# Attention and FFN on one core: score maxima on a finer grid and four units later, weight-conversion words in an idle output bank

## The chip, the cores and the metric

The kernel runs on one core of one Trainium2 chip. The metric is the time of the device for one execution, in microseconds (us). The kernel before was timed three times; the median counts. The profile is one execution, recorded by the hardware profiler.

## The reference

Attention over 4 batches of 8 heads, 768 tokens and 64 dimensions, in which a query sees only the keys of its hash bucket, and then an FFN over the 3072 tokens. Cut to what matters:

```python
q_bits = (einsum('bhsd,dk->bhsk', q, proj) > 0)          # 6 hash bits, k_bits the same
mask   = q_bucket[:, :, :, None] == k_bucket[:, :, None, :]
scores = where(mask, scale * q @ k.T, -1e9)
attn   = exp(scores - max(scores)); attn /= attn.sum() + 1e-9
x = (attn @ v).reshape(3072, 512)
h = x @ w_in                                            # 512 -> 2048
g = where(h >= 1, h, where(h <= -1, 0, (h + 1) ** 2 / 4))
out = g @ w_out                                         # 2048 -> 512
```

## The kernel before, in words

The 32 heads go one after another. A head has 12 units: two halves of 384 queries, each against six tiles of 128 keys. The mask is made part of the product: beside the parts of q and k the operand T2 holds rows for the hash bits and a row for the maximum, so that a score comes out of two matmuls (`s_unit`, L371 and L372) into one of four score tiles `s` in PSUM. Only the second, L372, reads T2. ScalarE takes the exponential twice (ph rounded, L380, and full, L385), and `lo_unit` subtracts them for the low part pl (L39), on VectorE, or on GpSimd (POOL) for units 0, 3, 6 and 9 of a head. Four units later `pv_unit` adds three matmuls with v (L404, L405, L406) into an output bank: bank 0 for the first half of a head (TensorE is at units 4 to 9 of the head), bank 1 for the second (units 10 to 15, the last four of which are units 0 to 3 of the next head). After the last unit of a half ScalarE copies the bank to xs (L412).

**Maxima.** For each head `max_mm` multiplies a tile of 128 rows of T2 with all 768 columns in a pair of matmuls (L310) into the one `smax` tile, which takes two banks of PSUM; VectorE reduces it (L314) to a column of nm. The next pair waits for that. A head has six pairs. In the loop a pair stands at the end of a unit, and its maximum follows the score matmuls of the next unit. From head 4 on there is a pair at the end of each even unit, for the head two ahead; the ends of the early pairs are in a table. When a head's six columns are there, `max_clamp` clamps nm in two steps on GpSimd (L342, L344), `max_tr` transposes it on TensorE into an output bank (L349), and `max_put` copies the result to te on ScalarE (L354) and sends it in two DMAs of SP's queue: into the row of T2 (L356) and to memory (L357). This happens in the head just before the one that reads the row: clamp at its unit 0, transpose at 4, copy and DMA at 5. Head 2 alone does it by halves of the queries (`half_clamp` on VectorE, `half_put`, L333 and L337).

**Hash bits.** For each pair of heads `bits_mm` (L210) makes two times four matmuls, one set in each output bank, ScalarE negates (L216), VectorE compares (L221), GpSimd scales, and at unit 18 of the pair `bits_put` sends four DMAs on SP's queue (L282) into T2.

**Weight conversion.** 24 pieces of the FFN's weights, 128x512 numbers of 64 bits each, are turned into float32 halves, one in each of heads 3 to 26 (`WeightSplit.steps`): a DMA (L62), a square on ScalarE (L69), and integer steps on VectorE, which build a word in the tile `wa` in SBUF: L70 (one input), L74, L78 (wraw and the word), L82 (the square times the word). Then a cast (L87), a subtraction and a DMA (L95). The offsets in `conv` set the unit of each step within the head.

All of it is one order of the program; each engine and SP's queue work through their instructions in that order. `tasks` holds what `at(unit, ...)` put at the end of a unit. Then comes the FFN, which this change does not touch: its weights keep `wa` in SBUF.

Of the kernel before, what the change touches and what calls it, by code (L numbers as in the profile page):

```python
# [41 lines left out]
class WeightSplit:  # L42
# [7 lines left out]
        nc.vector.memset(sc[:, 1:2], 29)  # L50
        self.sc = sc

    def steps(self, src, shape, hi, lo, cp, stage=None, low=None, keep=None):
        nc, n = self.nc, self.n
        st = {}

        def s0():
            st["raw"] = self.pool.tile([P, n, 2], I32, name="wraw")
            dst = st["raw"]
            if len(shape) == 4:  # L60
                dst = dst.rearrange("p (c f) t -> p c f t", c=shape[1])
            nc.sync.dma_start(out=dst, in_=src)  # L62

        def s1():
            raw = st["raw"]
            sq = st["sq"] = self.pool.tile([P, n], F32, name="wsq")
            a = st["a"] = self.pool.tile([P, n], I32, name="wa", bufs=1)
            high = raw[:, :, 1].bitcast(F32)
            nc.scalar.activation(out=sq, in_=high, func=AF.Square)  # L69
            nc.vector.tensor_scalar(out=a, in0=raw[:, :, 1], scalar1=0x07FFFFFF, scalar2=3,  # L70
                                    op0=ALU.bitwise_and, op1=ALU.logical_shift_left)

        def s2():
            nc.vector.scalar_tensor_tensor(out=st["a"], in0=st["raw"][:, :, 1], scalar=self.sc[:, 0:1],  # L74
                                           in1=st["a"], op0=ALU.bitwise_and, op1=ALU.bitwise_or)

        def s3():
            nc.vector.scalar_tensor_tensor(out=st["a"], in0=st["raw"][:, :, 0], scalar=self.sc[:, 1:2],  # L78
                                           in1=st["a"], op0=ALU.logical_shift_right, op1=ALU.bitwise_or)

        def s4():
            nc.vector.scalar_tensor_tensor(out=st["sq"], in0=st["sq"], scalar=WMIN2,  # L82
                                           in1=st["a"].bitcast(F32), op0=ALU.is_ge, op1=ALU.mult)
# [25 lines left out]
POOL_J = (0, 3)  # L109
PV_ORDER = (1, 2, 0, 4, 5, 3)  # L110
NU = 2 * NJ


def attention(ctx, tc, wst, T1, T2, qk, v, pj, cv, x_d, s_d, e_d, tasks, shared):
# [4 lines left out]
    shared["work"], shared["small"] = work, small  # L119
    ps_s = ctx.enter_context(tc.tile_pool(name="ps_s", bufs=4, space=PSUM))  # L120
    ps_o = ctx.enter_context(tc.tile_pool(name="ps_o", bufs=1, space=PSUM))
    ps_m = ctx.enter_context(tc.tile_pool(name="ps_m", bufs=1, space=PSUM))
# [138 lines left out]
                             start=True, stop=True)  # L261

    def row_half(hd, hf, bank=None):
        ps = ps_m.tile([P, 2, 512], F32, name="smax")[:, 0] if bank is None else obank[bank]
# [56 lines left out]
    def half_clamp(hd, hf):  # L321

        nm = nms[hd]
        x = nm[:, hf * HB:(hf + 1) * HB]
        nc.vector.tensor_scalar(out=nmh[:, hf, HB:2 * HB], in0=x, scalar1=CLAMP, scalar2=None, op0=ALU.is_gt)
        nc.vector.tensor_scalar(out=nmh[:, hf, 0:HB], in0=x, scalar1=CLAMP, scalar2=None, op0=ALU.min)

    def half_put(hd, hf, bank):
        pr, h = hd // 2, hd % 2
        if hf == 1:  # L330
            nms.pop(hd)
        ps = obank[bank]
# [4 lines left out]
        nc.sync.dma_start(out=T2[pr % NQK][7:8, 0, h, sl].bitcast(F32), in_=te[0:HB].bitcast(F32))  # L337
        nc.sync.dma_start(out=e_d[hd // H][hd % H:hd % H + 1, sl], in_=te[HB:2 * HB].bitcast(F32))
# [5 lines left out]
        eng.tensor_scalar(out=nm[:, 0:NJ], in0=nm[:, 0:NJ], scalar1=CLAMP, scalar2=None,  # L344
                          op0=ALU.min)

    def max_tr(hd, bank):
        ps = mx[hd] = obank[bank]
        nc.tensor.transpose(out=ps[0:2 * NJ, 0:P], in_=nms.pop(hd), identity=ident)  # L349

    def max_put(hd):
# [40 lines left out]

    xss = {}

    def pv_unit(n):
        hd, hf, jj = n // NU, (n % NU) // NJ, n % NJ
        j = PV_ORDER[jj]
        pr, h = hd // 2, hd % 2
# [3 lines left out]
        wa = va[:, j, h:h + 2, :].rearrange("p g d -> p (g d)")  # L402
        wb = vb[:, j, h:h + 2, :].rearrange("p g d -> p (g d)")
        nc.tensor.matmul(out=o, lhsT=wa, rhs=ph, start=(jj == 0), stop=False)  # L404
        nc.tensor.matmul(out=o, lhsT=wb, rhs=ph, start=False, stop=False)  # L405
        nc.tensor.matmul(out=o, lhsT=wa, rhs=pl, start=False, stop=(jj == NJ - 1))  # L406
        if jj == NJ - 1:
            if hf == 0:
# [121 lines left out]

    for t in (1, 0):
        at(0, first_scale, 1, t, nc.gpsimd)
    at(9, ones_row, 1, nc.vector)
    at(3, row_clamp, 0, NJ // 2, NJ)
    at(4, row_half, 0, 1, 1)
    for n, g in enumerate((1, 4, 5, 6)):
        at(g, quarter, n)
    at(6, lambda: nc.gpsimd.memset(T2[1][0:64, 0].bitcast(F32), 0.0))
    at(7, row_clamp, 1, 0, NJ // 2)
    for n in (0, 1):  # L540
        at(8, move, 1, n)
    at(8, bits_mm, 1, 0, 1)
    at(9, bits_cmp, 1, 0)
    at(9, row_half, 1, 0)
    at(9, row_flags, 0)
    at(10, bits_mm, 1, 1, 0)
# [54 lines left out]

    NG = NH * NU
    red = None
    early = {}
    for hd, gs in ((0, (0, 2)), (1, (4, 5, 6, 8, 11, 12)), (2, (15, 16, 17, 19, 20, 22)),
                   (3, (21, 23, 24, 26, 27, 29)), (4, (30, 31, 33, 34, 35, 37)),
                   (5, (38, 39, 41, 42, 44, 46))):
        early.update({n: (hd, NJ - len(gs) + i) for i, n in enumerate(gs)})
    for g in range(NG + LAG + 1):
        if g < NG:  # L610
            s_unit(g)
        if red is not None:
            max_red(*red)
            red = None
        if 1 <= g <= NG:
            lo_unit(g - 1)
        if g < 4 * NU:
            due = g in early
            hd, i = early.get(g, (0, 0))
        else:  # L620
            hd, i = g // NU + 2, g % NU // 2
            due = hd < NH and g % 2 == 0
        if g >= LAG and g - LAG < NG:
            pv_unit(g - LAG)
        if due:
            max_mm(hd, 2 * i)
            max_mm(hd, 2 * i + 1)
            red = (hd, i)
        for fn, a in tasks.pop(g, ()):
            fn(*a)  # L630
    for g in sorted(tasks):
        for fn, a in tasks[g]:
            fn(*a)
# [465 lines left out]
def lsh_attn_ffn(ctx: ExitStack, tc: tile.TileContext, qk, v, pj, cv, w_in, w_out, out):  # L1099
# [46 lines left out]
    def conv(g, steps, offs):  # L1146
        for fn, n in zip(steps, offs):
            at(g + n, fn)

    def wi_steps(i, cp, stage=None):  # L1150
        return ws.steps(win_v[:, :, i * P:(i + 1) * P, :], (P, NCT, P, 2), wih[i], wil[i], cp, stage, None, wq[i])

    def wo_steps(i, cp, stage=None, low=None):
        return ws.steps(wout_v[i], (P, DM, 2), woh[i], wol[i], cp, stage, low)
# [21 lines left out]
    attn = {}  # L1176
# [107 lines left out]
```

## Time and profile before

| | us |
|---|---|
| three runs | 980.84, 982.14, 981.41 |
| median | 981.41 |
| span of the profiled execution | 980.2 |
| TensorE busy in it | 966.7 |
| VectorE busy | 793.9 |
| ScalarE busy | 679.6 |
| GpSimd busy | 346.3 |

The profiled execution has a span of 980.2 us; its own time is one of the three runs' kind, between 980.84 and 982.14, so that about a microsecond lies around the span. The attention stage lasts to about 463 us, the FFN follows. In the rows PE is TensorE's matmuls, PEld its weight loads, DVE VectorE, ACT ScalarE, POOL GpSimd, SP SyncE. A row of a timeline gives start, duration, engine, line, operation, out<-in, and in brackets the idle time ahead with what ended it. A row of the waits gives who waited for whom, the total in us, how often, and the longest. A row of the groups gives count, busy time and the mean of one in ns.

### The profile page before, as it was taken

To read this page: it belongs to the slowest core of one execution; us is meant where nothing else is said; L and a number is where in the kernel's file an instruction comes from. 1 tells how busy PE (TensorE), PEld (TensorE's weight loads), DVE (VectorE), ACT (ScalarE), POOL (GpSimd) and SP (SyncE) were. 2 spreads that over 40 slices of the span, in tenths; PEclk is the share of its full clock that TensorE was granted. 3 is DMA by queue.
4 is the path that set the end of the run, shared out by engine and by line. 5 is a ranking of instruction groups with operands and counts; after the bars stand their busy time and mean duration, and the time that the engine had idled before them with its cause. 6 is when DMAs were issued, how large, how long until landed. Compare 5 with 4: busy or idle time off the path is not lost.

```text
span 980.2 us, 15590 instructions
## 1 busy us (share of the span) xinstructions
PE 966.7 (99%) x5050; PEld 889.7 (91%) x5050; DVE 793.9 (81%) x1359; ACT 679.6 (69%) x1481; POOL 346.3 (35%) x418
## 2 busy tenths in 40 slices
PE   8999999999999999999999999999999999999998
PEld 7889999999999999999999998888988889988886
DVE  8779999999999999887898887877866777655554
ACT  7878988898899898888655555455564545544444
POOL 8767777778887777666000000000000000000000
PEclk9999999999999999999999999999999999999999
DMA  6674667676666667644395478966458554454431
GB/s 164 178 189 108 165 175 184 192 180 192 168 159 162 177 174 187 161 119 126 126 319 185 129 237 287 314 223 205 116 157 240 149 183 119 143 159 119 117 88 65
DMA packets 95113, 167.56 MB, mean 171 GB/s; under 512 B 13956, under 2 KB 51960, under 8 KB 95032
## 3 DMA queue, kind: packets, MB, share of 16 engines
q1 hardware_dynamic: 94808, 166.56, 59.6%
q8 instruction: 40, 0.66, 0.3%
q14 instruction: 41, 0.34, 0.1%
q10 hardware_dynamic: 224, 0.00, 0.0%
HBM read 106.13 MB, written 33.87 MB: 143 GB/s over the span
## 4 chain that ended last, share of the span: by engine, by line
PE 87%; DVE 5%; ACT 3%; DMA 2%; issue 1%; POOL 1%; SPq 1%; DVEq 0%; ACTq 0%; POOLq 0%
PE y L822 27%; PE h L1054 18%; PE smax L310 7%; PE h L959 7%; PE o L406 5%; PE o L404 5%; PE o L405 5%; PE s L371 5%; PE s L372 5%; DVE nm L314 2%; PE o L210 2%; DVE pl L39 1%; DMA wraw<-in_w_in_dram 1%; ACT ph L380 1%; DMA sm<-sd 0%
## 5 line engine op out<-in xcount | busy, mean ns | idle before, releaser
L380 ACT ACTIVATE ph<-s 128x384 fp32r<-128x384 f32 x380 | 188.3, 496 | 41.1 <-PE s L372 35.1
L314 DVE TENSOR_REDUCE nm<-smax 128x1 f32<-128x768 f32 x189 | 179.0, 947 | 15.2 <-PE smax L310 13.6
L39 POOL TENSOR_TENSOR pl<-pf,ph 128x384 fp32r<-128x384 f32 x128 | 141.9, 1112 | 87.8 <-ACT pf L385 83.1
L787 DVE SCALAR_TENSOR_TENSOR t<-t 128x384 f32<-128x384 f32 x128 | 71.3, 557 | 101.6 <-ACT z L782 101.3
L39 DVE TENSOR_TENSOR pl<-s,ph 128x384 fp32r<-128x384 f32 x256 | 135.8, 544 | 10.8 <-ACT s L385 9.6
L371 PE MATMUL s<-t 128*128 128x384 f32 x384 | 132.2, 344 | 0.0
L404 PE MATMUL o<-ph,va 128*128 128x386 f32 x384 | 130.1, 339 | 1.1 <-DVE neg L221 1.1
L406 PE MATMUL o<-pl,va 128*128 128x386 f32 x384 | 130.1, 339 | 0.4 <-DVE pl L39 0.4
L405 PE MATMUL o<-ph,vb 128*128 128x386 f32 x384 | 130.1, 339 | 0.0
L372 PE MATMUL s<-t 128*128 128x384 f32 x384 | 129.3, 337 | 0.0
L385 ACT ACTIVATE s<-s 128x384 f32<-128x384 f32 x252 | 125.2, 497 | 0.0
L822 PE MATMUL y<-t,ghi 128*128 128x512 f32 x384 | 124.7, 395 | 0.0
L310 PE MATMUL smax<-t 128*128 128x384 f32 x378 | 103.1, 354 | 5.7 <-DVE nm L314 4.4
L781 ACT ACTIVATE t<-h,mh 128x384 f32<-128x384 f32 x56 | 32.6, 581 | 84.0 <-PE h L959 44.3
L310 PEld LDWEIGHTS smax<-t 128*128 128x128 f32 x378 | 64.4, 188 | 23.8 <-DVE nm L314 22.1
L792 ACT CAST ghi<-z 128x384 fp32r<-128x384 f32 x129 | 65.1, 505 | 30.1 <-DVE z L788 26.3
L782 ACT ACTIVATE z<-t,m 128x384 f32<-128x384 f32 x128 | 79.0, 617 | 4.2
L1054 PE MATMUL h<-wbig,t 128*128 128x384 f32 x399 | 81.4, 336 | 0.0
L822 PEld LDWEIGHTS y<-t,ghi 128*128 128x128 f32 x384 | 71.3, 188 | 11.1 <-ACT ghi L792 0.3
L1054 PEld LDWEIGHTS h<-wbig,t 128*128 128x128 f32 x399 | 71.6, 188 | 5.3
L781 ACT ACTIVATE t<-wsq,mh 128x384 f32<-128x384 f32 x48 | 29.6, 617 | 67.0 <-DVE wsq L1067 40.8
L822 PE MATMUL y<-t,glo 128*128 128x512 f32 x192 | 76.0, 396 | 0.0
(189 smaller groups left out, 2134.9 us busy)
## 6 DMA issues: line engine op xcount, KB each, us to landing
t<-wc SPq DMA_DIRECT2D x92, 256.0 KB
t<-t SPq DMA_DIRECT2D x60, 384.0 KB
wraw<-wc SPq DMA_DIRECT2D x76, 256.0 KB
raw<-in_qk_dram SPq DMA_DIRECT2D x14, 768.0 KB
wraw<-in_w_in_dram SPq DMA_DIRECT2D x16, 512.0 KB
wraw<-in_w_out_dram SPq DMA_DIRECT2D x16, 512.0 KB
t<-ed SPq DMA_DIRECT2D x36, 192.0 KB
xd<-xs SPq DMA_DIRECT2D x32, 192.5 KB
```

What stands on the lines that cost most here:

```text
L39: eng.tensor_tensor(out=out, in0=a, in1=b, op=ALU.subtract)
L310: nc.tensor.matmul(out=smax[hd][:, hf, 0:HS], lhsT=t2[:, 0, h, i * P:(i + 1) * P], rhs=t2[:, 1, h, hf * HS:(hf + 1) * HS], start=True, sto ...
L314: nc.vector.tensor_reduce(out=nmp(hd)[:, i:i + 1], in_=smax[hd][:, :, 0:HS], axis=AX.XY, op=ALU.max, negate=True)
L371: nc.tensor.matmul(out=ps[:, 0:HS], lhsT=t1[:, 1, h, ks], rhs=t1[:, 0, h, sl], start=True, stop=False)
L372: nc.tensor.matmul(out=ps[:, 0:HS], lhsT=t2[:, 1, h, ks], rhs=t2[:, 0, h, sl], start=False, stop=True)
L380: nc.scalar.activation(out=ph[:, 0:HS], in_=ps[:, 0:HS], func=AF.Exp, scale=SCALE)
L385: nc.scalar.activation(out=pf, in_=ps[:, 0:HS], func=AF.Exp, scale=SCALE)
L404: nc.tensor.matmul(out=o, lhsT=wa, rhs=ph, start=(jj == 0), stop=False)
L405: nc.tensor.matmul(out=o, lhsT=wb, rhs=ph, start=False, stop=False)
L406: nc.tensor.matmul(out=o, lhsT=wa, rhs=pl, start=False, stop=(jj == NJ - 1))
L822: nc.tensor.matmul(out=ys[c][m], lhsT=g_[:, m * P:(m + 1) * P], rhs=w, start=(first and k == 0), stop=(last and k == 2))
L1054: nc.tensor.matmul(out=ps, lhsT=w[:, cs], rhs=x, start=(n == 0 and s not in (2, 3, 6)), stop=(n == 5), skip_group_check=True)
```

## The change

Five things, in one step:

- The word of the conversions is no longer the tile `wa` in SBUF but output bank 0, read as integers, for the pieces that are converted in the attention stage. The bank is idle from unit 10 to 15 of a head, so the steps move: L70 and L74 to unit 10, L78 to 12, L82 to 14; the later steps one unit earlier.
- The hash products of a pair, from the third pair on, move from units 7 (bank 1) and 11 (bank 0) to units 5 and 7, both in bank 1.
- The pairs of the maxima of heads 1 to 5 are placed by slots, five to a unit (a slot is a score or output matmul), so that a pair may stand in the middle of a unit: heads 2 to 5 every 7.7 slots. From head 6 on they stay at the end of even units, four units later than before.
- Clamp, transpose and copy follow: from head 5 on at units 3, 6 and 7 of the head before; heads 2 to 4 go by halves, clamped on GpSimd. The transposes go into a score tile and no longer into an output bank.
- Two small moves at the start: `ones_row(1)` behind the first hash compare, `row_clamp(1)` one unit later.

The core of the diff:

```diff
-    def steps(self, src, shape, hi, lo, cp, stage=None, low=None, keep=None):
+    def steps(self, src, shape, hi, lo, cp, stage=None, low=None, keep=None, word=None):
...
-            a = st["a"] = self.pool.tile([P, n], I32, name="wa", bufs=1)
+            a = st["a"] = self.pool.tile([P, n], I32, name="wa", bufs=1) if word is None else word()
...
+    shared["work"], shared["small"], shared["word"] = work, small, lambda: obank[0].bitcast(I32)
...
-        nc.vector.tensor_scalar(out=nmh[:, hf, HB:2 * HB], in0=x, scalar1=CLAMP, scalar2=None, op0=ALU.is_gt)
-        nc.vector.tensor_scalar(out=nmh[:, hf, 0:HB], in0=x, scalar1=CLAMP, scalar2=None, op0=ALU.min)
+        nc.gpsimd.tensor_scalar(out=nmh[:, hf, HB:2 * HB], in0=x, scalar1=CLAMP, scalar2=None, op0=ALU.is_gt)
+        nc.gpsimd.tensor_scalar(out=nmh[:, hf, 0:HB], in0=x, scalar1=CLAMP, scalar2=None, op0=ALU.min)
...
-    def max_tr(hd, bank):
-        ps = mx[hd] = obank[bank]
+    def max_tr(hd, bank=None):
+        ps = mx[hd] = ps_s.tile([P, 512], F32, name="s") if bank is None else obank[bank]
...
+        between(3)
         nc.tensor.matmul(out=o, lhsT=wb, rhs=ph, start=False, stop=False)
+        between(4)
...
-    at(9, ones_row, 1, nc.vector)
...
+    at(9, ones_row, 1, nc.vector)
...
-    at(18, half_clamp, 2, 0)
-    at(19, half_put, 2, 0, 1)
-    at(23, half_clamp, 2, 1)
-    at(25, half_put, 2, 1, 0)
+    for hd, gs in ((2, (19, 21, 24, 26)), (3, (29, 31, 34, 36)), (4, (38, 40, 43, 45))):
+        for n, g in enumerate(gs):
+            at(g, half_put if n % 2 else half_clamp, hd, n // 2)
...
-        if 0 < hd < NH - 2:
-            gc, gt = ((g + NU + 6, g + NU + 7) if hd == 1 else (g + NU + 2, g + NU + 4) if hd == 2
-                      else (g + NU, g + NU + 4))
-            at(gc, max_clamp, hd + 2, nc.gpsimd if hd > 2 else nc.vector)
-            at(gt, max_tr, hd + 2, 1)
-            at(gt + (hd > 1), max_put, hd + 2)
+        if 2 < hd < NH - 2:
+            at(g + NU + SHIFT - 1, max_clamp, hd + 2, nc.gpsimd)
+            at(g + NU + SHIFT + 2, max_tr, hd + 2)
+            at(g + NU + SHIFT + 3, max_put, hd + 2)
...
-            bits_at = ((20, 1), (23, 0)) if pr == 0 else ((8 if pr == 1 else 7, 1), (11, 0))
+            bits_at = (((20, 1), (23, 0)), ((8, 1), (11, 0)))[pr] if pr < 2 else ((5, 1), (7, 1))
...
+    places = [5, 15] + [25, 33, 40, 48, 55, 62] + [80 + 77 * n // 10 for n in range(4 * NJ)]
...
+        early.update({5 * ((hd - 2) * NU + SHIFT + 2 * i + 1): (hd, i) for i in range(NJ)})
...
+        def between(k):
+            if 5 * g + k in early:
+                hd, i = early.pop(5 * g + k)
+                max_mm(hd, 2 * i)
+                max_mm(hd, 2 * i + 1)
+                if k == 5:
+                    return hd, i
+                max_red(hd, i)
...
-        conv((2 * i + 3) * NU, wi_steps(i, nc.scalar), (0, 7, 9, 13, 15, 17, 19, 21))
+        conv((2 * i + 3) * NU, wi_steps(i, nc.scalar), (0, 10, 10, 12, 14, 16, 18, 20))
...
-        conv((4 + 2 * n) * NU, first, (0, 7, 9, 13, 15, 16))
+        conv((4 + 2 * n) * NU, first, (0, 10, 10, 12, 14, 15))
```

`SHIFT` is 4. The order shows what this does to two engines. First VectorE in head 11, before: L314 is a maximum, pl the low parts, wa the word of the conversion.

```order
L70 TENSOR_SCALAR wa_2485<-wraw_2381 128x512
L39 TENSOR_TENSOR pl_6_168<-s_2474,ph_6_161 128x384
L314 TENSOR_REDUCE nm_2394<-smax_2497 128x1
L39 TENSOR_TENSOR pl_0_162<-s_2488,ph_0_155 128x384
L74 SCALAR_TENSOR_TENSOR wa_2485<-wraw_2381,wsc_108,wa_2485 128x512
L314 TENSOR_REDUCE nm_2394<-smax_2523 128x1
L39 TENSOR_TENSOR pl_2_164<-s_2514,ph_2_157 128x384
L39 TENSOR_TENSOR pl_3_165<-s_2526,ph_3_158 128x384
L314 TENSOR_REDUCE nm_2560<-smax_2546 128x1
L78 SCALAR_TENSOR_TENSOR wa_2485<-wraw_2381,wsc_108,wa_2485 128x512
```

The same place after (all lines in the changed file are up to six higher: L315 is the maximum, L70 to L82 are the same; o0 is output bank 0):

```order
L315 TENSOR_REDUCE nm_2457<-smax_2505 128x1
L39 TENSOR_TENSOR pl_0_162<-s_2496,ph_0_155 128x384
L70 TENSOR_SCALAR o0_137<-wraw_2395 128x512
L74 SCALAR_TENSOR_TENSOR o0_137<-wraw_2395,wsc_108,o0_137 128x512
L315 TENSOR_REDUCE nm_2457<-smax_2530 128x1
L39 TENSOR_TENSOR pl_2_164<-s_2521,ph_2_157 128x384
L39 TENSOR_TENSOR pl_3_165<-s_2537,ph_3_158 128x384
L78 SCALAR_TENSOR_TENSOR o0_137<-wraw_2395,wsc_108,o0_137 128x512
L315 TENSOR_REDUCE nm_2457<-smax_2557 128x1
L39 TENSOR_TENSOR pl_5_167<-s_2565,ph_5_160 128x384
L82 SCALAR_TENSOR_TENSOR wsq_2533<-wsq_2533,o0_137 128x512
L315 TENSOR_REDUCE nm_2457<-smax_2586 128x1
```

L70 and L74 now stand side by side ahead of one maximum, and L78 and L82 stand ahead of the next two.

Second SP's queue at the end of head 10 and in head 11, before: xd and sd take the finished output of a head, te is the row of the maxima, bits the hash bits.

```order
L416 DMA xd1_60<-xs_2336 64x770
L417 DMA sd1_64<-xs_2336 1x768
L95 DMA wq15_96<-wsq_2298 128x512
L356 DMA t2_0_77<-te_2453 1x6x128
L357 DMA ed1_68<-te_2453 6x128
L282 DMA t2_1_78<-bits_2308 8x768 x4
L62 DMA wraw_2549<-in_w_out_dram 128x1024
```

After (L419 is L416, L357 is L356, L283 is L282):

```order
L419 DMA xd1_60<-xs_2352 64x770
L420 DMA sd1_64<-xs_2352 1x768
L95 DMA wq15_96<-wsq_2368 128x512
L283 DMA t2_1_78<-bits_2282 8x768 x4
L357 DMA t2_0_77<-te_2492 1x6x128
L358 DMA ed1_68<-te_2492 6x128
L62 DMA wraw_2561<-in_w_out_dram 128x1024
```

The row of the maxima has moved from ahead of the four transfers of the hash bits to behind them.

More of the change, by code (lines that the diff above doesn't have):

```diff
@@ L111 @@
 NU = 2 * NJ
+SHIFT = 4
 def attention(ctx, tc, wst, T1, T2, qk, v, pj, cv, x_d, s_d, e_d, tasks, shared):
@@ L118, in attention @@
     small = ctx.enter_context(tc.tile_pool(name="asmall", bufs=2))
-    shared["work"], shared["small"] = work, small
+    shared["work"], shared["small"], shared["word"] = work, small, lambda: obank[0].bitcast(I32)
     ps_s = ctx.enter_context(tc.tile_pool(name="ps_s", bufs=4, space=PSUM))
@@ L263, in row_half @@
     def row_half(hd, hf, bank=None):
-        ps = ps_m.tile([P, 2, 512], F32, name="smax")[:, 0] if bank is None else obank[bank]
+        ps = ps_s.tile([P, 512], F32, name="s") if bank is None else obank[bank]
         row_mm(hd, hf, ps)
@@ L324, in half_clamp, with half_put @@
         x = nm[:, hf * HB:(hf + 1) * HB]
-        nc.vector.tensor_scalar(out=nmh[:, hf, HB:2 * HB], in0=x, scalar1=CLAMP, scalar2=None, op0=ALU.is_gt)
-        nc.vector.tensor_scalar(out=nmh[:, hf, 0:HB], in0=x, scalar1=CLAMP, scalar2=None, op0=ALU.min)
-    def half_put(hd, hf, bank):
+        nc.gpsimd.tensor_scalar(out=nmh[:, hf, HB:2 * HB], in0=x, scalar1=CLAMP, scalar2=None, op0=ALU.is_gt)
+        nc.gpsimd.tensor_scalar(out=nmh[:, hf, 0:HB], in0=x, scalar1=CLAMP, scalar2=None, op0=ALU.min)
+    def half_put(hd, hf):
         pr, h = hd // 2, hd % 2
@@ L331, in half_put @@
             nms.pop(hd)
-        ps = obank[bank]
+        ps = ps_s.tile([P, 512], F32, name="s")
         nc.tensor.transpose(out=ps[0:2 * HB, 0:P], in_=nmh[:, hf], identity=ident)
@@ L393, in attention, with pv_unit @@
     xss = {}
-    def pv_unit(n):
+    def pv_unit(n, between):
         hd, hf, jj = n // NU, (n % NU) // NJ, n % NJ
@@ L538, in attention @@
     at(6, lambda: nc.gpsimd.memset(T2[1][0:64, 0].bitcast(F32), 0.0))
-    at(7, row_clamp, 1, 0, NJ // 2)
+    at(8, row_clamp, 1, 0, NJ // 2)
     for n in (0, 1):
@@ L603, in attention @@
     red = None
[L604 to L608, printed above, removed]
-    for g in range(NG + LAG + 1):
+    order = [(0, 4), (0, 5)] + [(hd, i) for hd in range(1, 6) for i in range(NJ)]
+    places = [5, 15] + [25, 33, 40, 48, 55, 62] + [80 + 77 * n // 10 for n in range(4 * NJ)]
+    early = {n + (n % 5 == 1): hi for n, hi in zip(places, order)}
+    for hd in range(6, NH):
+        early.update({5 * ((hd - 2) * NU + SHIFT + 2 * i + 1): (hd, i) for i in range(NJ)})
+    for g in range(NG + LAG + 1):
+        def between(k):
[6 more added lines that the diff above has]
+                max_red(hd, i)
         if g < NG:
@@ L613, in attention @@
             max_red(*red)
-            red = None
         if 1 <= g <= NG:
             lo_unit(g - 1)
[L617 to L622, printed above, removed]
-        if g >= LAG and g - LAG < NG:
[L624 to L628, printed above, removed]
+        between(2)
+        if g >= LAG and g - LAG < NG:
+            pv_unit(g - LAG, between)
+        red = between(5)
         for fn, a in tasks.pop(g, ()):
             fn(*a)
+    assert not early
     for g in sorted(tasks):
@@ L1148, in conv, with word @@
             at(g + n, fn)
+    attn = {}
+    def word():
+        return attn["word"]()
     def wi_steps(i, cp, stage=None):
-        return ws.steps(win_v[:, :, i * P:(i + 1) * P, :], (P, NCT, P, 2), wih[i], wil[i], cp, stage, None, wq[i])
+        return ws.steps(win_v[:, :, i * P:(i + 1) * P, :], (P, NCT, P, 2), wih[i], wil[i], cp, stage, None, wq[i], word)
     def wo_steps(i, cp, stage=None, low=None):
-        return ws.steps(wout_v[i], (P, DM, 2), woh[i], wol[i], cp, stage, low)
+        return ws.steps(wout_v[i], (P, DM, 2), woh[i], wol[i], cp, stage, low, None, None if stage is None else word)
     woh = [hi for hi, lo in wo]
@@ L1175, in lsh_attn_ffn @@
     actx = ExitStack()
-    attn = {}
     for b in range(B - 1):
```

## The prediction

> **What bounds the kernel now.** I read the page first (busy time and the chain that ended last), then the waits of TensorE's weight loads in three stretches of the attention stage, then the timelines of one head. The page, busy time of each engine and the chain's share by engine:
>
> ```profile
> PE 966.7 (99%) x5050; PEld 889.7 (91%) x5050; DVE 793.9 (81%) x1359; ACT 679.6 (69%) x1481; POOL 346.3 (35%) x418
> ```
>
> ```profile
> PE 87%; DVE 5%; ACT 3%; DMA 2%; issue 1%; POOL 1%; SPq 1%; DVEq 0%; ACTq 0%; POOLq 0%
> ```
>
> TensorE is the bound; the change adds no matmul and removes none. It can only win back, or add, time in which TensorE waits. The waits of its weight loads, by line and releaser (total, times, longest), first from 14 to 79.6 us, then to 399.6, then to 463:
>
> ```profile
> PEld smax L310 <- DVE nm L314: 9.4, 17, 1.4
> PEld o L404 <- DVE neg L221: 1.4, 1, 1.4
> PEld smax L310 <- POOL t L247: 0.8, 1, 0.8
> ```
>
> ```profile
> PEld smax L310 <- DVE nm L314: 11.6, 39, 0.4
> PEld smax L310 <- DVE sm L666: 0.5, 1, 0.5
> ```
>
> ```profile
> PEld o L349 <- issue: 0.4, 1, 0.4
> ```
>
> Nearly all is one wait: a pair of score matmuls (L310) needs the only smax tile, which VectorE's maximum (L314) must have read. One head in detail, head 5 around its unit 10. VectorE, start and duration, whole stretch:
>
> ```profile
> 104.96 0.96 DVE L314 TENSOR_REDUCE nm<-smax 128x1 f32<-128x768 f32 x1
> 105.83 0.55 DVE L39 TENSOR_TENSOR pl<-s,ph 128x384 fp32r<-128x384 f32 x1
> 106.30 1.58 DVE L74 SCALAR_TENSOR_TENSOR wa<-wraw,wsc,wa 128x512 int32<-128x512 int32 x1
> 107.80 0.94 DVE L314 TENSOR_REDUCE nm<-smax 128x1 f32<-128x768 f32 x1
> 108.67 1.00 DVE L39 TENSOR_TENSOR pl<-s,ph 128x384 fp32r<-128x384 f32 x2
> 109.60 0.94 DVE L314 TENSOR_REDUCE nm<-smax 128x1 f32<-128x768 f32 x1
> 110.47 1.01 DVE L78 SCALAR_TENSOR_TENSOR wa<-wraw,wsc,wa 128x512 int32<-128x512 int32 x1
> ```
>
> The two pairs on TensorE in the same stretch, and the weight load of the second:
>
> ```profile
> 106.51 0.51 PE L310 MATMUL smax<-t 128*128 128x384 f32 x2
> ...
> 108.80 0.62 PE L310 MATMUL smax<-t 128*128 128x384 f32 x2
> ```
>
> ```profile
> 108.80 0.30 PEld L310 LDWEIGHTS smax<-t 128*128 128x128 f32 x2 [0.35 <-DVE nm L314]
> ```
>
> A pair can issue 0.06 after the maximum ends (108.74, 108.80). Unhindered, twelve matmuls stand from one pair to the next, 2.11 us, so the second was due at 108.62: it came 0.18 late and ran 0.11 longer. The word step L74 (1.58 here) sat ahead of the maximum. The wait listed at 0.35 cost TensorE 0.29, so I take 0.8 of the 12.1 us in the middle stretch, 9.7 us, as what its 23 conversion heads lose now, 0.42 each; and 0.9 of the early 11.6, 10.4 us.
>
> **The change part by part.** *Words in the output bank.* The four word steps now write PSUM (L82 reads it), and the first two stand together ahead of the maximum of unit 10. Their rows now (steady heads, then the later stage where GpSimd is idle; count, total, mean ns):
>
> ```profile
> L39 DVE TENSOR_TENSOR pl<-s,ph 128x384 fp32r<-128x384 f32 x184 | 96.9, 542 | 4.2 <-ACT s L385 4.2
> L78 DVE SCALAR_TENSOR_TENSOR wa<-wraw,wsc,wa 128x512 int32<-128x512 int32 x23 | 25.7, 1116 | 0.0
> L74 DVE SCALAR_TENSOR_TENSOR wa<-wraw,wsc,wa 128x512 int32<-128x512 int32 x24 | 25.2, 1050 | 0.0
> L82 DVE SCALAR_TENSOR_TENSOR wsq<-wsq,wa 128x512 f32<-128x512 f32 x23 | 24.8, 1080 | 0.0
> ```
>
> ```profile
> L221 DVE TENSOR_TENSOR neg<-o,neg 32x384 f32<-32x384 f32 x23 | 12.4, 541 | 5.7 <-ACT neg L216 5.7
> ```
>
> ```profile
> L74 DVE SCALAR_TENSOR_TENSOR wa<-wraw,wsc,wa 128x512 int32<-128x512 int32 x8 | 6.0, 752 | 0.3
> ```
>
> Beside a busy GpSimd L74, with two inputs in SBUF, takes 1050; alone it takes 752. The subtraction pl, with one input in PSUM, takes 542 beside the same GpSimd. So I expect 0.75 for each of L74, L78 and L82, three times 0.33 off VectorE per head. The Trainium skill's page "SBUF — State Buffer" (section "Who interferes with whom") says just this: two SBUF inputs contend with a GpSimd read, at most one does not; the rows above agree.
>
> How fast one follows another, from the later stage:
>
> ```profile
> 504.54 0.68 DVE L39 TENSOR_TENSOR wol<-wsq,woh 128x512 fp32r<-128x512 f32 x1
> 505.14 0.42 DVE L70 TENSOR_SCALAR wa<-wraw 128x512 int32<-128x512 int32 x1
> 505.60 0.75 DVE L74 SCALAR_TENSOR_TENSOR wa<-wraw,wsc,wa 128x512 int32<-128x512 int32 x1
> 506.27 0.62 DVE L846 SCALAR_TENSOR_TENSOR pcs<-tmp,xsvb,pcs 128x384 f32<-128x384 f32 x1
> ```
>
> From L70 to L74 0.46 us, from L74 to the next 0.67. L70 into PSUM is nowhere in the trace. Its ends: 0.46, if it stays as fast; 0.72, if it takes the 0.68 of L39 on as many elements and its 0.04 to the dependent step. I take 0.60, between them. The Trainium skill's page "VectorE: DVE Perf Modes" (section "Why PSUM operands drop a tier") says that a PSUM operand holds fp32 work to the plain rate; by it L70 would be at the 0.72 end and the sum 2.8 us higher. No run here shows it yet.
>
> L70 also gets a wait: the bank is free only when ScalarE has copied out the finished half of the head. That copy:
>
> ```profile
> 106.13 0.48 ACT L412 COPY xs<-o 128x384 f32<-128x384 f32 x1
> ```
>
> ends at 106.61, while VectorE is through with pl at 106.30. Behind the waiting L70 stand L74 and the maximum, and behind that TensorE's next pair. The walk, with the rows' times: L70 at 106.65, L74 at 107.25, maximum 107.91 to 108.87, pair at 108.93 where 108.62 was due: 0.31 late, and 0.1 for its longer run. Then VectorE is free at 108.78 (the next step starts 0.87 after a maximum's start), two pl take 0.93, L78 0.66, maximum 110.37 to 111.33, pair at 111.39 where 111.14 was due: 0.25 and 0.1. Then one pl, L82 and a maximum to 113.4, ahead of 113.6: no wait. That is 0.76 per head. In the heads that start a pair of heads, the second hash compare (L221, 0.54) now stands ahead of the maximum of unit 8, so that VectorE is later at L70; between 0 and 0.3 more, I take 0.14. Twelve odd heads at 0.76 and eleven even ones at 0.90 make 19.0 us against 9.7: **+9.3**. With L70 at its ends the odd heads pay 0.62 or 0.88: the total moves by -3.2 or +2.8.
>
> *The rows of the maxima.* From head 5 on, clamp, transpose and copy come later; for the transpose it is two units, 2.1 us. What follows it is ScalarE's copy te and two small transfers on SP's queue, and in odd heads the hash bits' four transfers now stand ahead of these. ScalarE, SP and TensorE in head 7:
>
> ```profile
> 129.77 0.25 ACT L354 CAST te<-o 12x128 fp32r<-12x128 f32 x1
> ```
>
> ```profile
> 130.05 0.77 SPq L356 DMA_DIRECT2D t<-te  x1
> ...
> 131.42 3.60 SPq L282 DMA_DIRECT2D t<-bits  x4
> ```
>
> ```profile
> 135.81 0.34 PE L372 MATMUL s<-t 128*128 128x384 f32 x1
> ```
>
> The row is issued 5.8 us ahead of the matmul that reads it. Two units later it would be 3.7 ahead; behind the bits' 3.6 us, if those start at 129.4, where SP is free, it is issued at 133.0, 2.8 ahead. The least that the trace shows to be in time:
>
> ```profile
> 396.34 1.54 SPq L356 DMA_DIRECT2D t<-te  x1
> ```
>
> ```profile
> 400.07 0.34 PE L372 MATMUL s<-t 128*128 128x384 f32 x1
> ```
>
> is 3.7. Each conversion wait ahead of the matmul gives the row 0.7 more, so I take no wait for most heads, and half a microsecond in the three whose queue also holds the sums' loads: **+1.5**. Its ends are 0 and, if the bits go no earlier than now, some 1.5 us in each of twelve odd heads less the 0.76 that the conversion gives, +9.
>
> *Heads 0 to 3.* Of 10.4 us, pairs set 7.7 matmuls apart against the 1.57 us that a pair and its maximum need (0.55 to the maximum, 0.96, 0.06) save most; the memset moved behind the hash compare saves about 0.7. What I leave: 1.3 at the start (0.8 of it the wait for POOL above), 0.5 at the hash compare, 1.2 in the tighter spacings, 1.3 where clamps now queue on POOL behind the low parts, 2.0 for the conversion of head 3. And one row comes later, the first half of head 2, transposed two units later:
>
> ```profile
> 41.55 1.13 SPq L337 DMA_DIRECT2D t<-te  x1
> ```
>
> ```profile
> 47.00 0.34 PE L372 MATMUL s<-t 128*128 128x384 f32 x1
> ```
>
> Its 5.45 us shrink by 2.1, and TensorE comes earlier: 0 to 4 us of wait, I take 2.0. Together 8.3 against 10.4: **-2.1**. The transposes in a score tile take away the 0.4 of L349, **-0.3**. The hash products in the other bank wait for nothing that is late, at nothing; if POOL's casts hold a bank, the cover is gone and each second one may cost 0.6.
>
> Sum: 9.3 + 1.5 - 2.1 - 0.3 = +8.4. The profiled execution's span is 980.2, its time among the three runs' 980.84 to 982.14; I add to the median of 981.41: **989.8 us**. A difference under 0.2%, 2 us, can't be told from none.
>
> **The rivals.** *Faster.* VectorE is quick enough: the copy is early or L70 does not lose by it, L70 takes 0.46 and the other words 0.60 each. Started at 106.30, the maximum ends at 108.32, before the pair is due; the second at 110.7, just when it is. Then the 9.7 go, with 2.1 of the early waits, and what shows next is the rows' lateness, uncovered, some 5 (twelve odd heads at 0.4): 981.4 - 9.7 - 2.1 - 0.3 + 5 = 974.3. For it speaks the contention that goes (1050 to 752), and that 23 waits are made of it; against it the copy's end at 106.61. It decides at L70 starting by 106.4 in most heads. Chance 0.25. *Flat.* The walk as above with L70 at 0.46 and no extra for even heads: 23 times 0.62 is 14.3, +4.6, all rows in time, so -4.1 early, and -0.3: 981.6. Chance 0.17. *Late rows.* The mechanism of the rows decides: it begins where the row's transfer is issued under about 2.8 us ahead of its matmul; with +9 instead of +1.5 the time is 997.3. For it speaks that the transfer now is behind four others and loads; against it that now it has 5.8 us. Chance 0.12. *The forecast*: 0.46, its own range 985 to 995 by L70's ends and the early terms.
>
> **How the numbers follow.** Slower takes the forecast and the late rows, 0.58; faster 0.25; same 0.17. The range leaves out 0.1 on each side: below 974 (the faster rival without the rows' lateness), above 998 (late rows with L70 at its slow end).
>
> **What would show it.** Right: in the waits of the weight loads smax <- nm grows from 11.6 to 18 or more us between 79.6 and 400 us, two waits per conversion head, at units 12 and 14; L74, L78 and L82 at 0.7 to 0.8 in the groups; L70 at 0.5 to 0.7, idle before it for xs. Late rows: waits of s for a DMA of te at the first unit of a head. Wrong: smax <- nm under 9 us in that stretch; then L70 started with the end of pl, or the words overlap more than the later stage shows.

## The result and the profile after

The changed kernel takes 998.3 us (median of 4 runs, 998.04 to 999.01), the kernel before 981.77 beside it: 1.0165 times as long, 95% interval 1.0151 to 1.0179. It is slower by 16.5 us, twice the 8.4 that was forecast and 0.3 us outside the range. The profiled execution has a span of 996.3 us against 980.2, 16.1 more. Among all runs below, one of the fifth experiment (1008.8 us at a granted clock of 0.988) is of a slower kind than the others and is left out of its time.

Busy time and the chain that ended last, after:

```profile
PE 969.4 (97%) x5052; PEld 890.8 (89%) x5052; DVE 778.8 (78%) x1351; ACT 679.0 (68%) x1483; POOL 319.9 (32%) x430
...
PE 70%; DVE 12%; ACT 11%; issue 3%; DMA 2%; POOL 0%; SPq 0%; ACTq 0%; DVEq 0%; POOLq 0%
```

VectorE has 15 us less to do and POOL 26 us less, and yet TensorE is held up more: in the chain VectorE's share (DVE) rises from 5% to 12% and ScalarE's (ACT) from 3% to 11%. The two matmuls more are transposes: heads 3 and 4 now go by halves too. The waits of the weight loads, first to 79.6 us, then from there to 408 us:

```profile
PEld s L373 <- DMA t<-te: 4.4, 1, 4.4
PEld o L211 <- ACT xs L415: 1.4, 1, 1.4
PEld smax L311 <- DVE nm L315: 1.2, 4, 0.7
```

```profile
PEld smax L311 <- DVE nm L315: 25.8, 46, 1.6
...
PEld s L373 <- DMA t<-te: 0.2, 1, 0.2
```

Early, the 9.4 us of waits for maxima are down to 1.2, but a new wait of 4.4 has come, and one of 1.4 just ahead of it. In the middle, 11.6 have become 25.8, in 46 waits: two in each of 23 heads. To place the difference, take each interval between the starts of two matmuls in TensorE's rows and count what it has over 0.175 us, where that is more than 0.06. By this count heads 0 to 3 lose 12.0 us (11.4 before), heads 4 to 26 lose 26.3 (11.7 before), the last five 3.5 (2.3 before). Together that is 16.4 us more, and the span grew by 16.1.

Here is head 5 after, VectorE around its unit 10, whole stretch, with ScalarE's copy and TensorE's pairs behind it:

```profile
107.79 0.55 DVE L39 TENSOR_TENSOR pl<-s,ph 128x384 fp32r<-128x384 f32 x1
108.54 0.70 DVE L70 TENSOR_SCALAR o<-wraw 128x512 int32<-128x512 int32 x1 [0.21 <-ACT xs L415]
109.28 0.76 DVE L74 SCALAR_TENSOR_TENSOR o<-wraw,wsc,o 128x512 int32<-128x512 int32 x1
109.94 0.95 DVE L315 TENSOR_REDUCE nm<-smax 128x1 f32<-128x768 f32 x1
110.81 1.01 DVE L39 TENSOR_TENSOR pl<-s,ph 128x384 fp32r<-128x384 f32 x2
111.74 0.75 DVE L78 SCALAR_TENSOR_TENSOR o<-wraw,wsc,o 128x512 int32<-128x512 int32 x1
112.39 0.95 DVE L315 TENSOR_REDUCE nm<-smax 128x1 f32<-128x768 f32 x1
```

```profile
108.02 0.49 ACT L415 COPY xs<-o 128x384 f32<-128x384 f32 x1
```

```profile
108.47 0.51 PE L311 MATMUL smax<-t 128*128 128x384 f32 x2
110.95 0.62 PE L311 MATMUL smax<-t 128*128 128x384 f32 x2 [0.22 <-DVE nm L315]
113.40 0.62 PE L311 MATMUL smax<-t 128*128 128x384 f32 x2
```

This is the forecast's walk, step for step: L70 waits for the copy, L74 and the maximum stand behind it, the pair due 2.11 after 108.47 starts at 110.95, 0.37 late, and the next one, 2.45 on, is late again. Only L70 is dearer than the 0.60 that was taken: 0.74 to the next step. The word steps in groups:

```profile
L74 DVE SCALAR_TENSOR_TENSOR o<-wraw,wsc,o 128x512 int32<-128x512 int32 x23 | 17.4, 756 | 0.8
L78 DVE SCALAR_TENSOR_TENSOR o<-wraw,wsc,o 128x512 int32<-128x512 int32 x23 | 17.1, 745 | 0.0
L70 DVE TENSOR_SCALAR o<-wraw 128x512 int32<-128x512 int32 x23 | 16.0, 695 | 5.0 <-ACT xs L415 4.9
L82 DVE SCALAR_TENSOR_TENSOR wsq<-wsq,o 128x512 f32<-128x512 f32 x23 | 15.5, 676 | 0.0
```

L74, L78 and L82 fell from 1050, 1116 and 1080 ns to 756, 745 and 676, as forecast; L70 rose from 547 to 695. All four are together 0.92 us shorter per head, and the two that stand side by side decide.

Three places were not foreseen, or not in their size or place. The first is the early row of head 2. SP's queue and TensorE there, the first rows behind the wait, and two stretches by engine (busy us of PE, PEld, DVE, ACT and POOL, then the granted clock, the DMA share and GB/s):

```profile
43.24 0.85 SPq L148 DMA_DIRECT2D raw<-in_qk_dram  x1
44.39 0.77 SPq L338 DMA_DIRECT2D t<-te  x1
```

```profile
49.49 0.69 PE L373 MATMUL s<-t 128*128 128x384 f32 x1 [4.05 <-DMA t<-te]
49.97 0.53 PE L405 MATMUL o<-ph,va 128*128 128x386 f32 x1
50.29 0.53 PE L407 MATMUL o<-ph,vb 128*128 128x386 f32 x1
```

```profile
49.20:53.00 3.80, 3.51 (x11) 3.51 (x12) 0.54 (x1) 2.51 (x5) 1.72 (x2) 0.50 0.95 209
53.00:60.00 7.00, 7.00 (x42) 6.67 (x40) 5.52 (x9) 5.58 (x14) 6.69 (x11) 0.99 0.24 48
```

The row, issued behind a load of 768 KB, is read 5.1 us after its issue, and for 3.6 us after the wait the granted clock is 0.50: matmuls stand 0.32 us apart where 0.175 is usual. Twelve times 0.145 is 1.7 us on top of the wait. The second is three heads (10, 18 and 26) that lose 2.1 us each where most lose 0.9. VectorE and POOL in head 10:

```profile
168.65 1.04 DVE L669 TENSOR_SCALAR sm<-sm 128x48 f32<-128x48 f32 x1
```

```profile
168.64 1.01 POOL L39 TENSOR_TENSOR pl<-pf,ph 128x384 fp32r<-128x384 f32 x1 [0.70 <-ACT pf L386]
```

A step on 48 columns (0.19 us in the kernel before, L667) lasts as long as the POOL instruction that started 0.01 us ahead of it, and it stands between a maximum and L78. The third is head 4, which also loses 2.1 us: there a pair of the finer grid waits for a maximum that stands behind L70, L74 and two low parts, words of head 3's conversion, and is 1.4 us late.

### The profile page after: what moved, and what is told of

Same layout as the page of the kernel before. It is cut to its first block, busy times and chain, and to the rows that moved or that the text cites. A ratio compares the mean times of both kernels' runs of the same rounds, so it can differ in the third digit from the quotient of the medians.

```text
span 996.3 us, 15611 instructions
## 1 busy us (share of the span) xinstructions
PE 969.4 (97%) x5052; PEld 890.8 (89%) x5052; DVE 778.8 (78%) x1351; ACT 679.0 (68%) x1483; POOL 319.9 (32%) x430
## 4 chain that ended last, share of the span: by engine, by line
PE 70%; DVE 12%; ACT 11%; issue 3%; DMA 2%; POOL 0%; SPq 0%; ACTq 0%; DVEq 0%; POOLq 0%
PE y L824 26%; PE h L1056 18%; PE h L961 7%; DVE nm L315 5%; PE smax L311 4%; ACT ph L381 3%; PE s L373 3%; PE s L372 3%; DVE pl L39 3%; PE o L409 3%; PE o L405 3%; PE o L407 3%; ACT pf L386 2%; ACT s L386 2%; DVE o L78 1%
## 5 line engine op out<-in xcount | busy, mean ns | idle before, releaser
L315 DVE TENSOR_REDUCE nm<-smax 128x1 f32<-128x768 f32 x189 | 180.2, 954 | 33.8 <-PE smax L311 32.2
L39 POOL TENSOR_TENSOR pl<-pf,ph 128x384 fp32r<-128x384 f32 x128 | 130.7, 1021 | 96.1 <-ACT pf L386 96.1
L794 ACT CAST ghi<-z 128x384 fp32r<-128x384 f32 x129 | 65.1, 505 | 30.1 <-DVE z L790 26.3
L373 PEld LDWEIGHTS s<-t 128*128 128x128 f32 x384 | 72.7, 189 | 4.8 <-DMA t<-te 4.6
```

The source lines that it names most:

```text
L39: eng.tensor_tensor(out=out, in0=a, in1=b, op=ALU.subtract)
L315: nc.vector.tensor_reduce(out=nmp(hd)[:, i:i + 1], in_=smax[hd][:, :, 0:HS], axis=AX.XY, op=ALU.max, negate=True)
L373: nc.tensor.matmul(out=ps[:, 0:HS], lhsT=t2[:, 1, h, ks], rhs=t2[:, 0, h, sl], start=False, stop=True)
```

## The experiments

The theory: the first two words side by side ahead of a maximum, with the bank's wait and L70's price into PSUM, make two late pairs in each conversion head. The rivals: the later maxima and their rows do it; or contention, or crowding as such.

**1. Words back in SBUF.**

```diff
-wih[i], wil[i], cp, stage, None, wq[i], word)        # and no word for the staged pieces
+wih[i], wil[i], cp, stage, None, wq[i])
-(0, 10, 10, 12, 14, 16, 18, 20)  (0, 10, 10, 12, 14, 15)
+(0, 7, 9, 13, 15, 17, 19, 21)    (0, 7, 9, 13, 15, 16)
```

> The changed kernel with one part undone: the words of the conversions are in SBUF again, at their old units 7, 9, 13 and 15. Theory (the four word steps in the bank, two of them side by side at unit 10, make the waits of the score maxima): heads 4 to 26 fall from 25 us of TensorE waits to about 12, and the time from 998.3 to 985 (983 to 988). Rival (the pairs four units later, with their clamps and transposes, make the waits themselves): the time stays at 995 or more.

991.9 us (1.0100 times before, 1.0078 to 1.0123): between the two. The waits from 79.6 to 408 us:

```profile
PEld smax L311 <- DVE nm L315: 9.6, 19, 1.7
PEld s L373 <- DMA t<-te: 8.5, 12, 1.3
```

The waits for maxima are back where they were, under the 11.6 of before. But 8.5 us of another wait appear, which the changed kernel has only for 0.2: the rows of the maxima come too late, once TensorE is no longer held up ahead of them. Both theory and rival hold in part: with the words undone the other four parts of the change still cost 10.2 us. One of these rows, issued behind three moves of q and k, is read 4.6 us after its issue (120.33 to 124.95 us) and is 1.1 us late.

**2. The words alone**, on the kernel before.

```diff
+words in obank[0], offsets (0, 10, 10, 12, 14, 16, 18, 20) and (0, 10, 10, 12, 14, 15)
+bits_at = (((20, 1), (23, 0)), ((8, 1), (11, 0)))[pr] if pr < 2 else ((5, 1), (7, 1))
+ps = mx[hd] = obank[bank] if hd < 5 else ps_s.tile([P, 512], F32, name="s")
```

> The kernel before with one part done alone: words in output bank 0 at units 10, 10, 12 and 14, the hash products at units 5 and 7 in the other bank (the bank has to be free) and the transposes from head 5 on in a score tile; score maxima where they were. Theory: some 0.5 us more in each of 23 conversion heads, 981.8 becomes 993 (990 to 996). Rival (the words alone are harmless, only their meeting with the later maxima costs): 985 or less.

992.1 us (1.0104, 1.0089 to 1.0119): the theory, within 1 us. The wait from 79.6 to 408 us:

```profile
PEld smax L310 <- DVE nm L314: 22.3, 46, 0.7
```

The same 46 waits, with every maximum where it had been. The words by themselves cost 10.4 us. So each half alone costs about 10 us, and both together 16.5. One row differs from the changed kernel, the second step of the sums (L667 here, L669 there):

```profile
L667 DVE TENSOR_SCALAR sm<-sm 128x48 f32<-128x48 f32 x3 | 0.6, 190 | 0.1
```

With the same words ahead of it and behind it, it takes 0.19 us here, and heads 10, 18 and 26 lose 1.25 us each, not 2.1.

**3. Head 2's maxima earlier.**

```diff
-places = [5, 15] + [25, 33, 40, 48, 55, 62] + [80 + 77 * n // 10 for n in range(4 * NJ)]
+places = [5, 15] + [25, 33, 40, 48, 55, 62] + [75, 80, 87] + [80 + 77 * n // 10 for n in range(3, 4 * NJ)]
-(2, (19, 21, 24, 26))
+(2, (18, 19, 24, 26))
```

> The changed kernel with the first three score maxima of head 2 at the ends of units 14 to 17 and its first half transposed at unit 19 instead of 21. Theory: the 4.1 us for which TensorE waits for that row go, and with them the half-rate matmuls behind it (12 at 0.32 instead of 0.175 us, with the wait 6.2 us in all): 998.3 becomes 992 (991 to 994). Rival (the row stands behind the loads on SP's queue and comes no earlier, or another row takes its place): 996 or more.

997.0 us (1.0156, 1.0134 to 1.0177): the rival. The 4.1 us wait became 1.0 and, for the second half row, 1.4. Part of the gain went to a standstill of VectorE at 22.6 to 26.7 us in the profiled execution, whose cause the trace does not show; the profiled run is the slowest of four, which spread from 995.5 to 998.8.

**4. First step in SBUF, the others in the bank.**

```diff
-            a = st["a"] = self.pool.tile([P, n], I32, name="wa", bufs=1) if word is None else word()
+            a = st["a"] = self.pool.tile([P, n], I32, name="wa", bufs=1)   # L74 then reads it and writes word()
-(0, 10, 10, 12, 14, 16, 18, 20)
+(0, 7, 10, 12, 14, 16, 18, 20)
```

> The changed kernel with the first word step L70 back in SBUF at unit 7, where it waits for no bank; the other three steps stay in the bank at units 10, 12 and 14 (the second reads the SBUF word). Theory (L70's 0.70 us into PSUM and its wait for the copy are what makes the first wait): waits per conversion head fall from 0.9 to 0.5 or less, the time to 989 (986 to 992). Rival (crowding by any three words at units 10, 12 and 14, or slow PSUM writes, makes them): 996 or more.

1009.5 us (1.0293, 1.0266 to 1.0319): slower than all others, by neither reason. The second step (L77 there), which now reads two SBUF tiles, from 79.6 to 408 us, then one of them and POOL beside it:

```profile
L77 DVE SCALAR_TENSOR_TENSOR o<-wraw,wsc,wa 128x512 int32<-128x512 int32 x23 | 37.8, 1642 | 5.7 <-ACT xs L418 5.7
```

```profile
95.37 2.10 DVE L77 SCALAR_TENSOR_TENSOR o<-wraw,wsc,wa 128x512 int32<-128x512 int32 x1 [0.18 <-ACT xs L418]
```

```profile
94.92 1.01 POOL L39 TENSOR_TENSOR vb<-vraw,va 128x384 fp32r<-128x384 f32 x1
95.89 1.02 POOL L39 TENSOR_TENSOR pl<-pf,ph 128x384 fp32r<-128x384 f32 x1
```

It takes 1642 ns where the form with one SBUF input takes 756: two POOL instructions end before it does. So the contention that the change removed is real, and it is what the bank buys; the forecast for this kernel left it out.

**5. Two units later instead of four**, on the first experiment's kernel.

```diff
-SHIFT = 4
+SHIFT = 2
-80 + 77 * n // 10
+80 + 73 * n // 10
```

> Words in SBUF at their old units (as in the first experiment), and the score maxima from head 6 on two units later instead of four, so that the transposes stand at unit 4 and the rows' transfers at unit 5, where they were before; the early maxima 7.3 matmuls apart instead of 7.7 to make room. Theory (with the conversion waits gone, the rows of the maxima come too late, 8.5 us of waits for their transfer in even heads): those waits go, 991.9 becomes 984 (982 to 986). Rival (the waits for the rows only give way to waits for the maxima, or the early stage holds the time): 989 or more.

991.6 us (990.9, 991.6 and 997.1; 1.0113, 1.0077 to 1.0148). The waits for rows after 79.6 us are gone, as the theory has it, but the time did not fall below the first experiment's 991.9: the rival. The waits from 79.6 to 408 us, and to 79.6:

```profile
PEld smax L311 <- DVE nm L315: 15.9, 35, 0.8
```

```profile
PEld s L373 <- DMA t<-te: 5.2, 1, 5.2
```

The 8.5 us gave way to 6.3 more for maxima (L78 took longer beside POOL, 1344 ns against 951 in the first experiment) and to an early stage in which heads 0 to 3 lose 16.0 us against 11.7, head 2's row 1.0 of it.

**6. The load behind head 2's row.**

```diff
-                at(g0 + 7, load_raw, pr + 3)
+                at(g0 + (7 if pr else 9), load_raw, pr + 3)
```

> The changed kernel with one load of q and k (768 KB, for the pair of heads 6 and 7) put two units later, so that on SP's queue it stands behind the first half row of head 2 and not ahead of it. Theory (the row's 4.9 us from issue to its matmul are the load ahead of it): the 4.1 us wait and the half-rate matmuls behind it shrink to 1 us or none, 998.3 becomes 993 (992 to 995). Rival (the row is late because it is transposed late): 997 or more.

997.5 us (1.0157, 1.0137 to 1.0177), in the profiled execution 994.1 against 996.3. The wait fell to 2.5 us, but the half rate stayed behind it. Both the load and the later transpose make the row late; the time agrees with the rival, the trace with half the theory.

**7. A short first step**, on the words alone.

```diff
-            nc.vector.tensor_scalar(out=a, in0=raw[:, :, 1], ...)
+            part = slice(0 if word is None else HS, n)
+            nc.vector.tensor_scalar(out=a[:, part], in0=raw[:, part, 1], ...)
```

> The words alone in the bank, as in the second experiment, with the first word step on 128 of its 512 columns (three quarters of it are left out). Its wait for the copy stays. Theory (L70's 0.74 us to the next step is what makes the first wait; 0.30 instead brings the maximum in time): waits per conversion head fall from 0.9 to 0.1 to 0.2, and the time from 992.1 to 976 (973 to 979). Rival (the wait for the bank alone, or the other three words, hold the maxima): 986 or more.

982.45 us (1.0004, 0.9994 to 1.0013), between the theory and the rival. L70 (L71 there) and the wait for maxima, both from 79.6 to 408 us:

```profile
L71 DVE TENSOR_SCALAR o<-wraw 128x128 int32<-128x128 int32 x23 | 6.8, 296 | 4.7 <-ACT xs L413 4.7
```

```profile
PEld smax L311 <- DVE nm L315: 10.8, 25, 0.7
```

0.40 us less in L70 takes 0.42 us off each of 23 heads (9.7 us against the 992.1 of the words alone): L70's time is on the path one for one, and the first wait of each head is gone, though L70 still waits for the copy (4.7 us in all). The second stayed, 0.35 with the pair's longer run, where 0.1 to 0.2 had been expected; it is as long as with the full L70, so L78 and two low parts fill that interval by themselves.

**8. Two mends**: the fifth and sixth experiments' edits together.

> The two-units-later kernel with the load put later as well. Theory: both mends add up, 984 less 5 is 979 (977 to 981), faster than the kernel before. Rival (the early row is late in any case): 983 or more.

998.4 us (1.0160, 1.0107 to 1.0213): the theory fails. Its runs lie between 990.6 at a granted clock of 1.0 and 1003.9 at 0.991, so nothing finer can be read from it.

**9. The wait filled** with matmuls of zeros.

```diff
+    def fill():
+        ps = ps_s.tile([P, 512], F32, name="s")
+        for _ in range(37):
+            keep_busy(ps)
+    at(23, fill)
```

> The changed kernel with 37 small matmuls of zeros (256 columns, into a score tile that nothing reads) at the end of unit 23, so that TensorE works through the 4.1 us in which it otherwise waits for the first row of head 2. Theory (the wait also halves the clock for the 3.6 us behind it): the wait stays in length, the matmuls of units 24 to 26 stand 0.175 instead of 0.32 us apart, and the time falls by 1.7 to 2 us, 998.3 to 996.4. Rival (the half rate has another cause, such as contention while the loads land): the spacing and the time stay, 998 or more.

998.3 us (1.0182, 1.0161 to 1.0203). TensorE behind the filled wait, the two stretches, and a wait that is new up to 80 us:

```profile
49.60 0.44 PE L373 MATMUL s<-t 128*128 128x384 f32 x1
49.88 0.34 PE L405 MATMUL o<-ph,va 128*128 128x386 f32 x1
50.06 0.33 PE L407 MATMUL o<-ph,vb 128*128 128x386 f32 x1
```

```profile
49.20:53.00 3.80, 3.80 (x21) 3.29 (x21) 1.76 (x3) 3.35 (x8) 1.85 (x2) 1.00 0.66 135
```

```profile
PEld s L334 <- POOL nmh L327: 1.1, 1, 1.1
```

The clock is 1.00 and the spacing 0.175, with the DMA as busy during the filling (share 0.91 from 44 to 49.2 us) as in the changed kernel (0.87): the wait, and not the loads, had halved the rate. Yet the time is the same. At unit 28 TensorE is 1.3 us ahead of the changed kernel, at unit 32 only 0.3: it meets the clamps of head 3's half row on POOL, which end 0.1 us earlier. The mechanism is shown; most of the gain is given back at the next late datum.

**10. The sums later.**

```diff
-        at(g + 15, xm.sums_add)
+        at(g + 18, xm.sums_add)
```

> The changed kernel with the sums' two steps on VectorE (three times in the attention stage) three units later. Theory (in heads 10, 18 and 26 they stand between the first two words' maximum and L78, and the second takes 1.04 us beside GpSimd, which costs 1.15 us in each): the waits of these heads fall from 2.1 to 0.95, the time by 3.4 us to 995. Rival (the step's 1.04 us moves with it and delays another maximum): 997.5 or more.

998.2 us (1.0177, 1.0155 to 1.0198): the rival. VectorE in head 10:

```profile
172.55 1.04 DVE L669 TENSOR_SCALAR sm<-sm 128x48 f32<-128x48 f32 x1
173.51 0.94 DVE L315 TENSOR_REDUCE nm<-smax 128x1 f32<-128x768 f32 x1
```

It meets POOL again, and delays the third maximum instead of the second: 1.95 us lost in each of the three heads, 2.1 without the edit.

**11. The copy first.**

```diff
+        if g % NU != LAG + NJ - 1:
+            s_exp()                  # the two exponentials of the unit
...
             pv_unit(g - LAG, between)
+        s_exp()                      # in that unit behind the copy
```

> The changed kernel with ScalarE's copy of the finished half ahead of the two exponentials of the same unit, so that the bank is free some 0.4 us earlier. Theory (L70 waits 0.21 us per head for that copy, and each such delay is on the path): the first wait of each conversion head shrinks from 0.4 to 0.2, 23 times 0.2 is 4.8 us, 998.3 becomes 993.5 (992 to 995). Rival (the exponentials, now later, delay the low parts and with them L70 or the output matmuls): 997 or more.

995.2 us (1.0138, 1.0123 to 1.0153), 3.1 us won of the 4.8. VectorE in head 4 (a maximum, a low part, L70, L74, a maximum, two low parts):

```profile
93.46 0.96 DVE L315 TENSOR_REDUCE nm<-smax 128x1 f32<-128x768 f32 x1
94.33 0.55 DVE L39 TENSOR_TENSOR pl<-s,ph 128x384 fp32r<-128x384 f32 x1
94.85 0.69 DVE L70 TENSOR_SCALAR o<-wraw 128x512 int32<-128x512 int32 x1
95.58 0.76 DVE L74 SCALAR_TENSOR_TENSOR o<-wraw,wsc,o 128x512 int32<-128x512 int32 x1
96.25 0.95 DVE L315 TENSOR_REDUCE nm<-smax 128x1 f32<-128x768 f32 x1
97.11 1.16 DVE L39 TENSOR_TENSOR pl<-s,ph 128x384 fp32r<-128x384 f32 x2
```

L70 waits no more. The first pair of a conversion head is late by 0.13 instead of 0.37, but the two low parts take 1.16 instead of 1.01, as their exponentials come later, and the second pair is late by 0.40 instead of 0.25. That is about 0.1 us per head; a like part of the gain comes from heads 10, 18 and 26, which lose 1.5 us instead of 2.1: the second step of the sums takes 0.19 us here, the first 0.72.

**12. Three mends**: the edits of 6, 10 and 11 on the changed kernel.

> The changed kernel with three mends: the load behind head 2's row, the sums three units later, the copy ahead of the exponentials. Theory: they add up, 998.3 less 1, 3.4 and 4.8 is 989 (987 to 992), still slower than the kernel before because the second wait of each conversion head (0.35 us) stays. Rival: 994 or more.

993.5 us (1.0120, 1.0105 to 1.0135): 4.8 us better than the change, half a microsecond from the rival's bound: of the three mends only the copy had clearly paid alone. No kernel of this study is faster than the one before.

## Why the prediction was right in direction and wrong in size

The mechanism named, the words in the bank, was there and close to its size. What failed is the rest of the sum, the moved maxima with their rows, clamps and transposes: it was put at -0.9 us (+1.5, -2.1 and -0.3) and measures about +6 on top of the words alone (998.3 against 992.1). Term by term, with the second experiment for the words and, for the rest, the time lost by heads in the changed kernel less that in the second experiment:

| term | forecast | measured |
|---|---|---|
| words in the bank | +9.3 | +10.4 |
| heads 0 to 3 | -2.1 | +0.8 |
| waits for rows, heads 4 to 26 | +1.5 | +0.2 |
| the sums' step, heads 10, 18 and 26 | none | +2.6 |
| head 4, behind the conversion of head 3 | (2.0 counted in heads 0 to 3) | +1.2 |
| what is left of heads 4 to 26 | none | +0.6 |
| the last five heads | -0.3 | +0.7 |
| sum | +8.4 | +16.5 |

These sizes say where the time is lost. They do not say that a mend in one place brings it back: the third, sixth, ninth and tenth experiments won at most 1.3 us each; only the copy put first won more (3.1).

**Words in the bank.** Two late pairs per head, at units 12 and 14, and three steps of 0.68 to 0.76. L70 was taken at 0.60 to the next step, between ends of 0.46 and 0.72; it measures 0.74, just above the upper end. The upper end was taken from another operation on as many elements, the lower from L70's own row in SBUF, and the Trainium skill's page "VectorE: DVE Perf Modes" (section "Why PSUM operands drop a tier") put L70 at the upper: 695 ns in PSUM against 419 in SBUF beside an idle POOL agrees with it. At 0.74 the walk gives 0.90 per odd head; 0.90 was measured with the words alone and 0.96 in the changed kernel. For even heads the forecast's 0.90 was right by luck: L70 cost 0.14 more, and the 0.14 for the hash compare did not come.

**The sums' step** was no term at all. Its price, 0.19 us before, hid that such a step can last as long as a POOL instruction that it meets. The working put that contention on steps with two inputs in SBUF; L669 has one, and in the trace of before L70, with one, was longer beside POOL too (419 alone, 547). The words did not bring it about, since with the words alone the step takes 0.19. In head 10 POOL's clamps stand at that place then; in the changed kernel they come later, and a low part starts just ahead of L669.

**Rows of the maxima.** The waits were 0.2: the conversion's waits gave the rows their time, as forecast. But the place was wrong: with the words back in SBUF the late rows are those sent in even heads, behind the moves of q and k, and not those sent in odd heads behind the hash bits. Their uncovered price was put at 5 in the faster rival; it measured 8.5, by which that rival's sum would be 977.8.

**Heads 0 to 3.** Head 2's row was sized at 2.0 in a range of 0 to 4; it costs 4.2 of wait and 1.7 of halved clock. Without these 5.9 the four heads lose 6.1 us, where 6.3 was left for them with the conversion of head 3, whose late pairs fall in head 4. That the row was issued ahead of a load before (41.55 and 44.02 us) and behind it now was not looked for, and the clock was not thought of.

**The last five heads.** The 24th conversion has its two late pairs in head 27, 0.95 us with 0.35 before. In head 30 output matmuls wait for low parts, 1.2 us with 0.3 before; the first experiment has these waits as well and the fifth, with maxima two units later, has not, so they belong to the shift by four units. How it delays the low parts was not followed.

The late rows, the rival at 997.3, gave nearly the measured time by a mechanism that did not act.

## What to carry to other kernels

When two steps on a side engine are put side by side ahead of one that the bound engine waits for, their sum decides and not the engine's total: here VectorE got 15 us less work and the kernel 16.5 us slower. A step's price belongs to where its operands lie and to what runs beside it, so an operation that is moved to another memory, and has no row there, is to be sized at its slower end. Before removing a wait, look at what the wait has been giving time to: behind several of these stood a later row, a clamp or a maximum that took the gain back.

## What the runs showed of the hardware

A TensorE that stood still for 4.1 us ran at half the granted clock for 3.6 us after it, and not where the wait was filled with matmuls. Half rate also followed waits of 3.0 us (third experiment) and 2.4 us (sixth, the clock at 0.67 over the 5.2 us behind it), but not the wait of 2.3 us for the same row in the eighth, whose profile has a clock of 1.00 throughout. In the first experiment's four runs the time rose as the granted clock fell: 989.5, 990.7, 993.1 and 993.2 us at 0.998, 0.996, 0.995 and 0.994. A VectorE step on 48 columns took 1.04 us instead of 0.19 when a POOL instruction of 1.01 us had started just ahead of it. Word steps with two SBUF inputs took 1642 ns in the fourth experiment, 1050 to 1116 in the kernel before and 752 where POOL is idle; with one input in PSUM they took 676 to 756 beside a busy POOL.
